# A fused long convolution and gated MLP: weights kept in an idle buffer, a complex product combined on VectorE, and whole-tile transfers

## Chip, cores, metric

One core of one Trainium2 chip runs the whole program. The metric is the device time of one execution in microseconds (us), lower is better. A profile is one execution; its span is about 2 us shorter than the time of the same execution. Runs are compared within one chip session, where kernel and kernel before alternate.

## The reference, cut to what matters

```python
# q, k, v: 1 x 2048 x 640 bf16; w_gate, w_up: 640 x 1728; w_down: 1728 x 640
x  = A_q
xn = layernorm(x)
k_shift = sum of 4 shifted copies of k, each times a weight per channel
kv = k_shift * v
y  = irfft(rfft(pad(kv)) * rfft(pad(ssm_k)))[:2048] + kv * ssm_D   # causal convolution of length 2048
glu = (sigmoid(xn @ w_gate) * (xn @ w_up)) @ w_down
out = x + xn * y + glu
```

The 2048 rows lie in the kernel as 16 row groups of 128 partitions (`acc[128, 16, 640]`). The gated MLP runs in four blocks of 512 rows: gate and up matmuls first, then the "down projection" of the block. The convolution is a Fourier transform in factors, all of them matmuls, done for ten channel steps, woven between the MLP's matmuls: first transform, second transform, a complex product in frequency on VectorE, third transform into a buffer V, and, after each five steps, a fourth transform out of V, whose result is multiplied with xn and added to `acc`.

## The kernel before

The instruction order is a fixed list made ahead of time (`ORDER`), so an edit of one operation leaves all others in their places. The parts that matter (cuts marked `# ...`):

```python
xq4 = A_q.flatten_outer_dims().rearrange("(n q m) d -> q n m d", q=4, m=NQ)   # 4 x 32 x 16 x 640
oq4 = out.flatten_outer_dims().rearrange("(n q m) d -> q n m d", q=4, m=NQ)

def load_x(q, m0, m1, eng, pri):            # a quarter of the partitions
    dma(lambda e: e.dma_start(acc[32 * q:32 * q + 32, m0:m1, :], xq4[q][:, m0:m1, :]), ...)

def store(m0, m1, pri, two=False):
    for q in range(4):
        dma(lambda e, q=q: e.dma_start(oq4[q][:, m0:m1, :], acc[32 * q:32 * q + 32, m0:m1, :]), ...)

def rec_prod(idx, pri):                     # X: spectrum of kv, H: of the filter; real part in partitions
    # ...                                   # 0-63, imaginary in 64-127; b = two halves of the step
    for h in range(2):                      # Q = X * (H with its halves swapped): four half products
        for b in range(2):
            a, o = slice(64 * h, 64 * h + 64), slice(64 - 64 * h, 128 - 64 * h)
            dve(... nc.vector.tensor_tensor(Q(b)[a], X(b)[a], H(b)[o], ALU.mult) ...)
    for b in range(2):                      # X = X * H
        dve(... nc.vector.tensor_tensor(X(b), X(b), H(b), ALU.mult) ...)

def rec_st3(idx, pri):                      # third transform: the sums and signs of the complex
    # ...                                   # product are in the two matrices A[0], A[1]
        nc.tensor.matmul(o, lhsT=tl[S_][:, b, 0, j, :], rhs=Ab[:, 0, :], start=True, stop=False)
        nc.tensor.matmul(o, lhsT=tl[Z][:, b, j, :], rhs=Ab[:, 1, :], start=False, stop=True)

for q in range(2):                          # first rows of x on two queues, SP and ACT
    load_x(q, 0, 1, "SP", FIX)
    load_x(q + 2, 0, 1, "ACT", FIX)
# ... rows 1-3 likewise; rows 4-7 and 8-15 later, four quarters each on SP
store(0, 8, 240.0); store(8, 12, 242.0); store(12, 14, 244.0); store(14, 15, 246.0); store(15, 16, 248.0)
```

Of the kernel before, what the change touches and what calls it, by code (L numbers as in the profile page):

```python
# [25 lines left out]
G = 4  # L26
# [16 lines left out]
def _dft_tables():  # L43
# [20 lines left out]
    A = np.zeros((2, K2, 2, N2, 2))  # L64
# [3 lines left out]
    A = A.reshape(P, 2, N2 * 2)  # L68
# [10 lines left out]
    6, 0, 5, 1, 4, 2, 8, 7, 11, 10, 13, 12, 9, 14, 3, 16, 71, 72, 15, 73, 74, 75, 17, 91, 86, 76, 77, 87, 81, 88, 19,  # L79
    78, 82, 64, 96, 79, 89, 83, 550, 97, 80, 90, 92, 84, 94, 147, 85, 93, 29, 98, 100, 99, 102, 101, 103, 148, 551,  # L80
    149, 150, 151, 154, 152, 63, 153, 156, 542, 155, 20, 157, 56, 543, 544, 546, 545, 24, 21, 547, 548, 27, 26, 552,
    549, 568, 553, 554, 556, 555, 57, 557, 558, 569, 560, 42, 559, 561, 562, 62, 564, 563, 23, 61, 565, 566, 32, 570,
    567, 572, 18, 571, 59, 574, 573, 104, 575, 586, 105, 578, 587, 106, 107, 588, 579, 576, 58, 108, 112, 582, 577,
    580, 43, 583, 111, 581, 30, 109, 589, 110, 25, 590, 584, 113, 39, 591, 593, 44, 45, 592, 132, 60, 134, 133, 22,
    594, 135, 596, 31, 585, 598, 597, 595, 600, 599, 602, 601, 604, 35, 603, 40, 605, 28, 36, 41, 158, 606, 159, 160,
    607, 37, 161, 610, 608, 609, 33, 611, 34, 38, 162, 612, 163, 164, 613, 171, 616, 628, 166, 615, 180, 614, 617,
    182, 181, 629, 618, 165, 622, 167, 168, 623, 66, 170, 177, 169, 65, 624, 179, 185, 172, 625, 67, 178, 174, 619,
    68, 627, 194, 626, 620, 621, 646, 630, 195, 196, 631, 632, 173, 647, 175, 197, 633, 634, 184, 199, 176, 47, 635,
    198, 183, 53, 636, 638, 200, 114, 50, 186, 639, 117, 46, 637, 54, 640, 201, 642, 49, 115, 187, 116, 51, 188, 191,
    641, 644, 643, 664, 193, 215, 189, 648, 192, 202, 649, 52, 190, 121, 214, 48, 650, 224, 203, 118, 665, 651, 119,  # L90
    652, 226, 225, 653, 213, 654, 136, 120, 205, 656, 655, 122, 129, 657, 216, 128, 69, 645, 227, 658, 218, 127, 217,
    95, 660, 228, 55, 659, 204, 661, 229, 219, 682, 662, 666, 220, 130, 244, 684, 206, 126, 243, 683, 668, 667, 663,
    207, 70, 246, 670, 669, 123, 247, 283, 124, 208, 290, 672, 288, 671, 230, 209, 289, 231, 287, 674, 125, 232, 286,
    233, 284, 675, 676, 234, 235, 210, 678, 211, 673, 677, 679, 212, 131, 680, 685, 221, 687, 686, 681, 223, 137,
    689, 138, 222, 688, 142, 245, 238, 717, 140, 690, 718, 248, 236, 239, 691, 693, 249, 237, 273, 139, 694, 143,
    250, 144, 145, 254, 141, 695, 255, 256, 696, 257, 697, 276, 698, 699, 258, 259, 700, 260, 275, 261, 240, 701,
    262, 242, 263, 702, 241, 274, 264, 705, 265, 703, 251, 704, 706, 146, 252, 253, 711, 303, 692, 712, 304, 305,
    713, 292, 277, 714, 278, 279, 294, 306, 293, 707, 716, 307, 295, 708, 280, 715, 308, 297, 266, 296, 268, 710,
    267, 298, 281, 719, 309, 269, 310, 720, 721, 311, 285, 709, 270, 312, 735, 723, 271, 313, 724, 314, 272, 722,
    725, 736, 727, 323, 726, 300, 729, 728, 301, 302, 282, 731, 324, 730, 333, 733, 291, 380, 732, 334, 335, 384,  # L100
    381, 737, 734, 753, 336, 739, 738, 338, 337, 383, 741, 299, 386, 740, 319, 743, 385, 742, 322, 320, 321, 387,
    745, 325, 330, 747, 744, 746, 331, 327, 326, 749, 332, 748, 328, 754, 317, 751, 391, 315, 329, 318, 390, 750,
    316, 349, 339, 356, 340, 755, 341, 400, 342, 757, 343, 756, 771, 402, 344, 772, 752, 759, 401, 806, 758, 389,
    347, 761, 392, 382, 345, 348, 394, 760, 346, 393, 395, 763, 762, 350, 396, 765, 420, 764, 419, 351, 388, 766,
    767, 352, 422, 773, 353, 423, 768, 769, 354, 357, 770, 774, 355, 358, 370, 776, 775, 359, 360, 778, 361, 777,
    403, 779, 781, 362, 780, 782, 405, 404, 783, 406, 377, 363, 407, 788, 378, 379, 789, 408, 371, 409, 790, 410,
    411, 372, 791, 373, 374, 784, 792, 793, 416, 375, 785, 417, 418, 794, 376, 427, 787, 795, 428, 429, 796, 786,
    421, 364, 797, 424, 365, 425, 800, 799, 367, 366, 412, 426, 368, 808, 807, 413, 449, 824, 414, 369, 810, 798,
    801, 415, 450, 452, 802, 453, 397, 803, 398, 399, 809, 451, 430, 804, 514, 811, 521, 805, 812, 432, 431, 813,
    814, 454, 460, 455, 825, 815, 816, 461, 462, 817, 818, 456, 433, 528, 819, 535, 820, 434, 435, 821, 822, 842,  # L110
    436, 437, 463, 438, 826, 439, 464, 440, 827, 465, 441, 823, 828, 442, 829, 444, 443, 830, 466, 445, 843, 467,
    831, 832, 468, 469, 446, 834, 470, 447, 471, 835, 448, 833, 836, 472, 837, 474, 473, 838, 475, 839, 840, 860,
    861, 476, 841, 844, 477, 478, 845, 846, 457, 847, 848, 458, 459, 849, 850, 482, 851, 852, 483, 484, 853, 854,
    862, 485, 855, 856, 486, 487, 857, 858, 488, 489, 479, 490, 863, 481, 480, 864, 865, 492, 498, 491, 866, 867,
    500, 499, 870, 868, 493, 869, 501, 859, 871, 502, 503, 872, 496, 494, 497, 876, 504, 495, 505, 877, 506, 507,
    873, 508, 878, 509, 510, 874, 875, 512, 511, 882, 513, 883, 536, 884, 537, 885, 538, 539, 879, 886, 887, 515,
    881, 880, 888, 540, 516, 541, 889, 517, 518, 905, 908, 890, 519, 907, 904, 891, 520, 906, 522, 903, 893, 892,
    909, 523, 902, 911, 524, 525, 910, 913, 526, 529, 912, 527, 530, 895, 894, 531, 532, 897, 533, 896, 534, 898,
    899, 900, 901
]  # L120
ON_DVE = [
    101, 134, 133, 135, 160, 181, 196, 226, 137, 138, 140, 139, 144, 256, 259, 253, 305, 302, 335, 337, 321, 360,
    404, 379, 374, 418, 429, 366, 399, 431, 462, 435, 478, 459, 484, 487, 480, 499, 503, 539, 518, 525, 532
# [93 lines left out]
def kernel(  # L217
# [42 lines left out]
    At = cst.tile([P, 2, 2 * N2], U16, name="At")  # L260
# [7 lines left out]
    eps = cst.tile([P, 1], F32, name="eps")  # L268
    st = cst.tile([P, 6, NQ], F32, name="st")
    eps2 = cst.tile([P, 1], F32, name="eps2")  # L270
# [6 lines left out]
    SLOTS = {"w": 4, "xq": 2, "xnT": 1, "sig": 2, "bs": 2, "kt": 1, "vt": 1, "ht0": 1, "ht1": 1, "kvt": 2,  # L277
# [12 lines left out]
    def make(b, tag, i):  # L290
        shape, dt = SHAPE[tag]
        if b.startswith("pst"):
            shape, dt = [P, NC, P], BF16
        if b.startswith("psT"):
            shape, dt = [P, 2, 1024], BF16
        if b in ("xk", "xv"):
            shape, dt = [P, 2, 2, 4 * DM // 2], BF16
        pool = ps if tag in ("c", "g") else wk
        return pool.tile(shape, dt, name=f"{tag}{i}", tag=f"{tag}{i}")
# [19 lines left out]
    def dma(fn, nd, run, q="SP", **kw):  # L319
        few = 1.4 if nd <= 64 and run > 1000 else 1.0  # L320
        plan.op({q: (0.48 + nd / 8000.0, lambda: fn(nc.sync if q == "SP" else nc.scalar))},
                size=few * nd * (10.6 + run / 23.8) / 16e3 + 0.03, **kw)

    def mm(n):
        return n / 2.4 + 3.0
# [4 lines left out]
               WDS=1.98, X1=22.54, X2=60.0, X3=84.74, LN1=40.0, LN2=80.0, LN3=90.0, WL=12.23, KV1=30.0,  # L330
               A1=53.98, LS1=55.48, LNS=70.0, EVB=-0.5, ST4=2.0, GP=2, H0=29.0, B0=64.19, SP=30.34)
# [15 lines left out]
    def load_x(q, m0, m1, eng, pri):  # L347
        dma(lambda e: e.dma_start(acc[32 * q:32 * q + 32, m0:m1, :], xq4[q][:, m0:m1, :]), 32, 1280 * (m1 - m0), q=eng,
            w=[("acc", m, q) for m in range(m0, m1)], pri=pri)

    def load_w(tr, n, pri):
        b = f"w{tr}_{n}"
        nb = max(0.0, pri - 14)
        kw = dict(pri=pri, nb=nb)
        if n == 6:
            dma(lambda e: e.dma_start(tl[b][:, :, 0:192], wgr[:, :, 1536:1728]), 640, 384, w=[(b, 0)], alloc=[(b, "w")], **kw)
            dma(lambda e: e.dma_start(tl[b][:, :, 256:384], wur[:, :, 1536:1664]), 640, 256, w=[(b, 1)], **kw)
            dma(lambda e: e.dma_start(tl[b][:, :, 192:256], wur[:, :, 1664:1728]), 640, 128, w=[(b, 2)], **kw)
            return
        f0, src = 512 * (n // 2), (wgr, wur)[n % 2]  # L360
        if tr == 0 and n < 2:
            for h in range(2):
                dma(lambda e, h=h: e.dma_start(tl[b][:, :, 256 * h:256 * h + 256], src[:, :, f0 + 256 * h:f0 + 256 * h + 256]),
                    640, 512, w=[(b, h)], alloc=[(b, "w")] if h == 0 else (), pri=pri + 0.5 * h)
# [520 lines left out]
```

## Time and profile before

| | kernel before |
|---|---|
| time, median of 3 | 277.43 us (276.89 to 512.8; the 512.8 is one stray execution) |
| span of the profiled execution | 279.1 us (that execution took 281.0) |
| TensorE busy / VectorE busy | 252.7 / 207.0 us |
| from the last matmul to the end | 12.3 us (10.9 in a second profile, taken later) |

How to read it: TensorE is busy for nearly the whole span, so what counts is each microsecond in which TensorE waits or has not yet begun or is already done. The prediction below prints the lines that carry this.

### The profile page before, as it was taken

The numbers are of one execution on the slowest core, as the hardware profiler recorded it, in microseconds if no ns is written. First come the engines' busy times: TensorE is split into PE (matmuls) and PEld (weight loads), VectorE is DVE, ScalarE is ACT, GpSimd is POOL, SyncE is SP. The second block draws the span as 40 slices with busy tenths as digits, with TensorE's granted clock in tenths as the row PEclk, the third lists the DMA queues.
The fourth block names the chain that finished last, engine by engine and source line by source line (L and its number), as shares of the span: only waits on it lengthen the run. The fifth ranks groups of instructions, "written<-read, shape, count | busy, mean of one in ns | idle before, by whom it ended". The sixth has DMA issues, their size and how long they took to land.

```text
span 279.1 us, 9682 instructions
## 1 busy us (share of the span) xinstructions
PE 252.7 (91%) x4344; PEld 156.5 (56%) x4380; DVE 207.0 (74%) x342; ACT 144.0 (52%) x214; POOL 0.7 (0%) x6
## 2 busy tenths in 40 slices
PE   8899887997799999999999999999999999999800
PEld 3754334774355547777456646667655555776500
DVE  5433147899489998869979998999888568864840
ACT  4642586133699979436557654224457754341100
POOL 1000000000000000000000000000000000000000
PEclk9999997999799999999999999999999999999965
DMA  7999999999769984999987602900464110000266
GB/s 181 265 234 290 193 202 192 152 273 256 148 132 338 193 218 115 166 216 152 250 168 209 162 2 67 295 25 5 116 194 167 44 31 2 2 2 2 63 132 188
DMA packets 94720, 42.17 MB, mean 151 GB/s; under 512 B 68432, under 2 KB 93592, under 8 KB 94360
## 3 DMA queue, kind: packets, MB, share of 16 engines
q1 hardware_dynamic: 94488, 41.24, 65.5%
q8 instruction: 34, 0.56, 0.9%
q10 hardware_dynamic: 192, 0.33, 0.4%
q14 instruction: 6, 0.05, 0.1%
HBM read 35.00 MB, written 5.24 MB: 144 GB/s over the span
## 4 chain that ended last, share of the span: by engine, by line
PE 83%; issue 4%; ACT 3%; DMA 3%; DVE 2%; SPq 1%; DVEq 0%; ACTq 0%
PE g L730 34%; PE g L745 23%; PE c L514 8%; PE c L582 4%; PE c L493 3%; PE c L552 3%; PE c L551 3%; DMA acc<-in_A_q_dram 3%; PE g L775 2%; PE g L710 2%; ACT jk L615 1%; ACT jk L621 1%; ACT xnT L312 1%; SPq L366 0%; DVE xq L652 0%
## 5 line engine op out<-in xcount | busy, mean ns | idle before, releaser
L730 PE MATMUL g<-xnT,w 128*128 128x512 bf16 x484 | 116.3, 384 | 4.6 <-issue 2.1
L730 PEld LDWEIGHTS <-w 128*128 128x128 bf16 x520 | 48.5, 99 | 56.8 <-issue 3.3
L745 PE MATMUL g<-wd,hT 128*128 128x320 bf16 x448 | 67.7, 304 | 0.1
L698 DVE TENSOR_TENSOR hT<-sig,g 128x512 bf16<-128x512 bf16 x52 | 35.4, 687 | 25.8 <-PE g L730 17.8
L745 PEld LDWEIGHTS <-hT 128*128 128x128 bf16 x448 | 42.4, 99 | 17.3 <-issue 0.4
L696 ACT ACTIVATE sig<-g 128x512 bf16<-128x512 f32 x52 | 30.8, 596 | 27.8 <-PE g L730 26.1
L312 ACT CAST S<-c 128x1024 bf16<-128x1024 f32 x25 | 24.8, 1012 | 21.8 <-PE c L514 21.8
L536 DVE TENSOR_TENSOR P<-S 64x1024 bf16<-64x1024 bf16 x40 | 27.4, 686 | 8.2 <-PE c L552 3.7
L514 PEld LDWEIGHTS <-Mt 64*128 64x128 f16 x1280 | 19.9, 95 | 10.5 <-issue 9.3
L312 ACT CAST V<-c 128x1024 bf16<-128x1024 f32 x20 | 19.4, 1013 | 11.5 <-PE c L552 11.5
L514 PE MATMUL c<-T,Mt 64*128 64x64 bf16 x1280 | 22.3, 190 | 2.9 <-issue 2.9
L313 DVE CAST S<-c 128x1024 bf16<-128x1024 f32 x15 | 18.3, 1223 | 5.5 <-PE c L514 5.4
L315 ACT ACTIVATE T<-c 128x1024 bf16<-128x1024 f32 x14 | 13.9, 1022 | 15.6 <-PE c L493 15.6
L551 PE MATMUL c<-At,S 128*128 128x128 f16 x160 | 19.3, 219 | 0.0
L552 PE MATMUL c<-At,P 128*128 128x128 f16 x160 | 19.3, 219 | 0.0
L312 ACT CAST T<-c 128x1024 bf16<-128x1024 f32 x14 | 13.8, 1014 | 10.6 <-PE c L493 10.5
L551 PEld LDWEIGHTS <-S 128*128 128x128 bf16 x160 | 15.6, 98 | 1.3 <-DVE S L539 0.2
L552 PEld LDWEIGHTS <-P 128*128 128x128 bf16 x160 | 15.6, 98 | 1.2
L756 DVE TENSOR_TENSOR acc<-g,acc 128x320 bf16<-128x320 f32 x32 | 14.5, 485 | 0.9 <-PE g L745 0.7
L458 DVE TENSOR_TENSOR tb<-kt,sT 128x1024 bf16<-128x1024 bf16 x20 | 13.7, 687 | 0.7 <-ACT kt L312 0.6
L463 DVE TENSOR_TENSOR ta<-ta,tb 128x1024 bf16<-128x1024 bf16 x20 | 13.8, 688 | 0.3
L539 DVE TENSOR_TENSOR S<-S 128x1024 bf16<-128x1024 bf16 x20 | 13.1, 688 | 0.3
(76 smaller groups left out, 196.1 us busy)
## 6 DMA issues: line engine op xcount, KB each, us to landing
w<-in_B_w_gate_dram SPq DMA_DIRECT2D x11, 640.0 KB, 4.8
w<-in_B_w_up_dram SPq DMA_DIRECT2D x11, 640.0 KB, 6.8
kt<-in_A_k_dram SPq DMA_DIRECT2D x8, 320.0 KB, 7.6
vt<-in_A_v_dram SPq DMA_DIRECT2D x8, 320.0 KB, 7.1
xnd<-xq SPq DMA_DIRECT2D x4, 640.0 KB, 7.5
ht<-in_A_ssm_k_dram SPq DMA_DIRECT2D x16, 96.0 KB, 6.3
wd<-in_B_w_down_dram SPq DMA_DIRECT2D x3, 480.0 KB, 5.5
acc<-in_A_q_dram SPq DMA_DIRECT2D x4, 320.0 KB, 7.3
```

What stands on the lines that cost most here:

```text
L312: fa = lambda: nc.scalar.copy(out=out_fn(), in_=in_fn())
L313: fd = lambda: nc.vector.tensor_copy(out_fn(), in_fn())
L315: fa = lambda: nc.scalar.activation(out_fn(), in_fn(), ACT.Copy, scale=scale)
L514: nc.tensor.matmul(tl[cs[e]][:, b, 64 * kk:64 * kk + 64], lhsT=Mb[rows, k, 64 - 64 * r:192 - 64 * r], rhs=tl[T][rows, 2 * k + r].rearrange ...
L536: dve(n, 2, lambda a=a, o=o, b=b: nc.vector.tensor_tensor(Q(b)[a], X(b)[a], H(b)[o], ALU.mult), r=sr + ([(Z, b, 0)] if h else []), w=[(Z, ...
L551: nc.tensor.matmul(o, lhsT=tl[S_][:, b, 0, j, :], rhs=Ab[:, 0, :], start=True, stop=False)
L552: nc.tensor.matmul(o, lhsT=tl[Z][:, b, j, :], rhs=Ab[:, 1, :], start=False, stop=True)
L696: act(512, lambda: nc.scalar.activation(tl[sg][:], tl[cs[0]][:], ACT.Sigmoid), r=[(cs[0],)], w=[(sg,)], alloc=[(sg, "sig")], pri=pri - 2000)
L698: dve(512, 1, lambda: nc.vector.tensor_tensor(hT[:, fc, :], tl[sg][:], tl[cs[1]][:], ALU.mult), r=[(cs[1],), (sg,)], w=[(hk, fc)], pri=pri ...
L730: nc.tensor.matmul(tl[c][:], lhsT=tl[wb][:, k, o:o + P], rhs=tl[X][:, k, :], start=(k == 0), stop=(k == NC - 1))
L745: nc.tensor.matmul(tl[pd[i]][:, 0:320], lhsT=hT[:, fc, t4 * P:(t4 + 1) * P], rhs=wd[:, fc, 320 * i:320 * i + 320], start=(fc == 0), stop=( ...
L756: dve(320, 1, lambda i=i, m=m, pd=pd: nc.vector.tensor_tensor(acc[:, m, 320 * i:320 * i + 320], tl[pd[i]][:, 0:320], acc[:, m, 320 * i:320 ...
```

## The change

Its intent, in five parts:

1. **Third transform halved.** VectorE forms the real and imaginary part of the product itself, so one matmul with a third matrix is enough: 160 matmuls less on TensorE, 40 "combining" instructions more on VectorE.
2. **VectorE relieved elsewhere.** In seven of ten steps two DMAs swap H's halves, so that four half products become two full ones; 18 gate products get their up value copied out of PSUM by ScalarE first.
3. **Weights kept.** The first block's gate and up weights stay on chip for the second block, four of their seven pieces in the buffer V. V is then free for the third transform only when the second block is done, and the order moves the second and third transforms back.
4. **Another end.** The last down block stands after the fourth transform and is split by column halves.
5. **Transfers joined.** Each load and store of `acc` is one DMA over 128 partitions in place of four over 32.

The core of the diff (the two order tables, the single-slot second transform and bookkeeping of keys are cut):

```diff
-    A = np.zeros((2, K2, 2, N2, 2))
+    A = np.zeros((2, K2, 3, N2, 2))
+    A[0, :, 2, :, 0], A[0, :, 2, :, 1] = c, s
+    A[1, :, 2, :, 0], A[1, :, 2, :, 1] = -s, c
 ...
-    def load_x(q, m0, m1, eng, pri):
-        dma(lambda e: e.dma_start(acc[32 * q:32 * q + 32, m0:m1, :], xq4[q][:, m0:m1, :]), 32, ...
+    def load_x(m0, m1, eng, pri):
+        dma(lambda e: e.dma_start(acc[:, m0:m1, :], xq4[:, :, m0:m1, :]), P, ...
+    def weight(tr, n):
+        tr = 0 if tr == 1 else tr
+        if tr == 0 and n < 4:
+            return ("wv", n), lambda: tl["wv"][:, n]        # lies in the slot of V
 ...
+        if idx in PRM["SWAP"]:                              # steps 3 to 9
+            for h in range(2):
+                dma(... tl[Z][a] <- tl[S_][o, :, 1] ...)    # H with its halves swapped
+            for b in range(2):
+                dve(... nc.vector.tensor_tensor(Q(b), X(b), Q(b), ALU.mult) ...)
 ...
+        if idx in PRM["ZC"]:                                # all ten steps
+            for b in range(2):
+                dve(... nc.vector.tensor_tensor(X(b)[0:64], X(b)[0:64], X(b)[64:P], ALU.subtract) ...)
+                dve(... nc.vector.tensor_tensor(X(b)[64:P], Q(b)[0:64], Q(b)[64:P], ALU.add) ...)
 ...
-   nc.tensor.matmul(o, lhsT=tl[S_][:, b, 0, j, :], rhs=Ab[:, 0, :], start=True, stop=False)
-   nc.tensor.matmul(o, lhsT=tl[Z][:, b, j, :], rhs=Ab[:, 1, :], start=False, stop=True)
+   nc.tensor.matmul(o, lhsT=tl[S_][:, b, 0, j, :], rhs=Ab[:, 2 if zc else 0, :], start=True, stop=zc)
 ...
+            parts = ([(0, 7, (0,)), (7, 14, (0,)), (0, 7, (1,)), (7, 14, (1,))] if last else ...
 ...
-    def store(m0, m1, pri, two=False):
-        for q in range(4):
-            dma(lambda e, q=q: e.dma_start(oq4[q][:, m0:m1, :], acc[32 * q:32 * q + 32, m0:m1, :]), 32, ...
+    def store(m0, m1, pri, d0=0, d1=DM):
+        dma(lambda e: e.dma_start(oq4[:, :, m0:m1, d0:d1], acc[:, m0:m1, d0:d1]), P, ...
 ...
-    store(15, 16, 248.0)
+    store(15, 16, 247.0, d1=320)
+    store(15, 16, 248.0, d0=320)
```

## The prediction

> **What bounds the kernel now.** I read the engine totals and slices first, then the chain of waits, the groups, the tail in order of time, and last the order in which both kernels place their instructions.
>
> ```profile
> PE 252.7 (91%) x4344; PEld 156.5 (56%) x4380; DVE 207.0 (74%) x342; ACT 144.0 (52%) x214; POOL 0.7 (0%) x6
> ...
> PEclk9999997999799999999999999999999999999965
> ...
> PE 83%; issue 4%; ACT 3%; DMA 3%; DVE 2%; SPq 1%; DVEq 0%; ACTq 0%
> ```
>
> TensorE carries 83% of the chain that ended last, so it is the bound; VectorE is second with 74%. The clock row shows two dips, near 45 and 72 us. A busy PE is not yet an efficient one, so I added up its work at the measured pace, from the end of the first block (14.65 us) on: gate/up 520 x 0.216 = 112.2 us, down 448 x 0.136 = 60.8, first transform 9.7, second 20 x 1.04 = 20.8, third 320 x 0.056 = 17.8, fourth 16 x 0.62 = 9.9, small ones 1.6; in all 232.8. TensorE ends at 266.8, so 252.1 us passed and 19.3 were lost: 11.6 of them before the 195th gate/up matmul (91.2 us). Those are the gaps at 29, 35, 40, 43 and 45 us (3.4), one of 2.92 at 68.25, and 9% of clock over 40 to 80 us (3.6); the rest is small. From 91 to 208 us (the 435th gate/up matmul) TensorE had 116 us of work in 117.
>
> ```profile
> L536 DVE TENSOR_TENSOR P<-S 64x1024 bf16<-64x1024 bf16 x40 | 27.4, 686 | 8.2 <-PE c L552 3.7
> L313 DVE CAST S<-c 128x1024 bf16<-128x1024 f32 x15 | 18.3, 1223 | 5.5 <-PE c L514 5.4
> L551 PE MATMUL c<-At,S 128*128 128x128 f16 x160 | 19.3, 219 | 0.0
> L552 PE MATMUL c<-At,P 128*128 128x128 f16 x160 | 19.3, 219 | 0.0
> L539 DVE TENSOR_TENSOR S<-S 128x1024 bf16<-128x1024 bf16 x20 | 13.1, 688 | 0.3
> ```
>
> These are the parts that the change touches: two matmuls per channel step in the third transform, and the complex product on VectorE. The 219 ns is one matmul's latency; 32 of them run from 243.11 to 244.90 us, 0.056 each.
>
> ```profile
> 259.35 16.29 SPq L598 DMA_DIRECT2D out_dram<-acc  x20
> ...
> 263.97 0.84 PE L582 MATMUL c<-V,Bt 32*32 32x80 bf16 x63 [0.75 <-ACT kt L312]
> ...
> 266.12 0.69 PE L582 MATMUL c<-V,Bt 32*32 32x80 bf16 x65 [1.32 <-issue]
> ...
> 268.70 0.82 DVE L591 TENSOR_TENSOR acc<-acc,vt 128x1280 bf16<-128x1280 bf16 x1
> ```
>
> The tail: TensorE stops at 266.8 and the last VectorE add at 269.5, yet the span is 279.1. Twenty stores, of 32 partitions each, leave one queue in order until 275.6, and the last needs 2.4 us to land. So 12.3 us follow the last matmul.
>
> **What the Trainium skill says.** "TensorE: Matmul & The Clock Gate", Back-to-back issue gap, gives N/2.4 + 2.5 ns, 56 ns at 128 columns; the trace has 0.056 us, so a matmul taken out is worth that, not 219 ns. "VectorE: DVE Perf Modes", The perf-mode tier table, says that a bf16 product reaches 2x from SBUF and 1x from PSUM; the trace agrees: 1024 columns from SBUF take 686 ns and 512 from PSUM 687. The same page, Two Vector instructions with no wait between them, says that an instruction whose inputs start in different quadrants of partitions waits for all earlier ones. The trace agrees: plain 1024-column products start every 0.60 us (128.43, 129.03, 129.63), four L536 half products, whose two inputs lie in different halves, take 2.83, so 0.71 each.[...]
>
> **Part 1, the third transform.** It goes from 320 matmuls to 160: 160 x 0.056 = 8.9 us off TensorE, which is the bound. The price is on VectorE: 40 half-partition combining operations with inputs in different halves, 40 x 0.71 = 28.4 us.
>
> **Part 2, relief for VectorE.** Counted in the two instruction orders: in 7 of 10 steps a copy by DMA swaps the halves, so 28 half products become 14 full ones: 28 x 0.71 - 14 x 0.60 = 11.5 us off. The S casts on VectorE go from 15 to 2, against three V casts more: 10 x 1.14 = 11.4 off (start to start). 18 gate products read SBUF in place of PSUM; from 819 ns at 1280 columns and 687 at 1024 I get 0.52 ns a column and so 0.42 us for 512, an estimate, which saves 18 x 0.26 = 4.8, less 0.7 for one copy. Small casts and norms give some 2 us back and take as much. Net 28.4 - 11.5 - 11.4 - 4.1 = +1.4: VectorE stays near 208 us. ScalarE gains 13 S casts (13.2), 17 copies (10) and loses some V casts: 144 to about 165 us, still no bound.
>
> **Part 3, weights kept.** Seven loads, 4.4 of 42.2 MB, vanish from the second block. But only 0.8 us of TensorE's waiting names a weight load, so directly it is worth about 1 us. It costs order: V is free for the third transform only after the second block. The first third-transform matmul moves from behind gate/up matmul 200 to behind 250, and the second transform starts behind 195 in place of inside the first down projection. The same convolution work must fit into less time. Of the 11.6 us lost early I expect 8 to stay; the 2.92 gap names no releaser, so I do not take all of it off.
>
> **Part 4, the middle, where I expect the new bound.** Between gate/up matmuls 195 and 435 the new order has, on VectorE: 61 key-value operations x 0.60 = 36.6, 15 gate products 9.0, 11 short ones 3.9, 12 half products 8.5, 25 full ones 15.5, 28 combining 19.6, 13 casts 14.8, 16 down adds 6.7, the fourth transform's 10 operations 7.9, small 0.9: 123.4 us. Before, the same stretch held 106.7 (in 117, 91%). TensorE there has 117.8 us plus about 25 switches from the second transform back to gate/up at the 0.16 us that the timeline shows: 122. The two engines are level, and neither can then be quite full. I take 96% of the longer: 128 us. Single-slot second transforms (32 matmuls, one PSUM slot, one cast) let this interleave; they change no work.
>
> **Part 5, the end.** The last 56 down matmuls (7.6 us) now stand after the fourth transform, whose stalls (2.2 us in the last 4.7) and adds no longer close the kernel, and stores are 6 in place of 20. After the last matmul remain one add 0.49, an issue 0.43, landing 2.4 and the close 1.1, with waits 4.6 us in place of 12.3: 7.7 off.
>
> **Sum.** Up to gate/up matmul 195: start 14.65 + work 60.1 (42.1 gate/up, 15.2 down, 1.3 first transform, 1.5 small) + 8 lost = 82.7. Middle 128: 210.7. From there TensorE has 45.9 us and I allow 3 for the fourth transform's stalls: 259.6. End 4.6: span 264.2. The profiled span of before was 279.1 against a median of 277.43 unprofiled, so 1.7 less: 262.5, rounded up to 263, 5% faster.
>
> **Rivals.** (a) TensorE stays the only bound: the middle takes 122 and early loss falls to 5. Then 254. For it: before, TensorE was 99% full there with VectorE at 91%. Against: VectorE now has 16% more to do in it. (b) VectorE becomes a hard bound, because the swap copies arrive late. A 320 KB read back takes 4.0 us here, and the swap (two of 256 KB on the one in-order queue) stands between the last cast and the product; if VectorE waits 1.5 us in each of 7 steps, the middle takes 138: 272, near no gain. For: queue waits of 12 and 36 us exist in that queue. Against: two S buffers, and next step's eight key-value products can fill the time. (c) The early part is bound by DMA anyway (busy share around 1.0 up to 60 us) and nothing is won before 83 us: +3, 266. (d) Tail alone: the parts in the middle cancel (8.9 off TensorE against VectorE's load) and only 8 to 10 us of the end remain: 268.
>
> **Range and chances.** The tail's 7.7 us and the 8.9 off TensorE are counted, not argued; the middle's filling is the wide term, from -6 to +10. Range 255 to 271. Faster by over 2% means under 271.9: 0.88. Within 2%: 0.11. Slower by over 2%: 0.01, only if the swaps or one wait stall everything.
>
> **What would show it.** Third transform: 160 matmuls, about 9 us of start-to-start time. VectorE busy 203 to 213, ScalarE 160 to 170. VectorE's share in 85 to 210 us above 92% while TensorE shows gaps ended by it (S casts, combining products); gate/up matmul 435 near 211. After the last matmul under 5.5 us. Wrong if VectorE idles on the swap copies, if gate/up 195 comes after 88 us, or if TensorE remains 99% full in the middle.

## More of the kernel before

For the kernel before, the rows that touch `acc` (destination and source, queue, count, size of one, median time from issue to landing in us):

```profile
acc<-in_A_q_dram SPq DMA_DIRECT2D x4, 320.0 KB, 7.3
out_dram<-acc SPq DMA_DIRECT2D x4, 320.0 KB, 5.5
acc<-in_A_q_dram SPq DMA_DIRECT2D x4, 160.0 KB, 7.2
...
acc<-in_A_q_dram ACTq DMA_DIRECT2D x2, 120.0 KB, 3.5
acc<-in_A_q_dram ACTq DMA_DIRECT2D x2, 40.0 KB, 2.0
acc<-in_A_q_dram SPq DMA_DIRECT2D x2, 40.0 KB, 1.8
```

All of `acc` goes in and out in quarters of 32 partitions, and the slowest group lands in 7.3 us. The page's DMA row (40 slices of the span, busy tenths of the 16 DMA engines) is

```profile
DMA  7999999999769984999987602900464110000266
```

It begins with 7 tenths, and its last two slices, in which little but stores runs, have 6.

## The result and the profile after

| | before | after |
|---|---|---|
| time, median | 277.62 us (4 runs) | 315.5 us (4 runs, 312.58 to 318.69) |
| ratio of fast runs | | 1.134, 95% interval 1.124 to 1.144 |
| span of the profiled execution | 279.1 us | 316.8 us |

A ratio is the mean time of one kernel's fast runs over the mean of the other's in the same rounds, so not quite the ratio of the medians. The profiled execution of after (318.69 us) counts as slow, being 2% above the fastest; I use its trace only for differences far larger than that. The prediction, 263 us and 88% for faster, was wrong in sign: by the means of the fast runs (314.5 against 277.4 us) the kernel is 37 us slower.

From the page of after, engine totals and the DMA row:

```profile
PE 260.8 (82%) x4220; PEld 153.9 (49%) x4220; DVE 206.4 (65%) x359; ACT 163.1 (51%) x241; POOL 0.7 (0%) x6
...
DMA  4699959725996537668979878121374520012221
```

VectorE's 206.4 and ScalarE's 163.1 us lie inside the predicted 203 to 213 and 160 to 170: the count of engine work was right. What differs is the row's two ends. It begins with 4 tenths in place of 7, and in the last slices, where only stores run, 2 tenths or fewer are busy in place of 6. The waits of after (engine, line and tile, what it waited for: us in all, times, longest):

```profile
ACT jk L642 <- DMA acc<-in_A_q_dram: 31.7, 3, 15.2
...
DVE bs L635 <- DMA acc<-in_A_q_dram: 11.8, 1, 11.8
...
PE c L701 <- DVE xq L679: 7.1, 1, 7.1
```

Three engines wait, directly or through one another, for the loads of x. In order of time (start, duration, engine, what, and in brackets the idle time before it and what ended that), the start, the load of rows 8 to 15, and the end:

```profile
15.76 0.72 PE L701 MATMUL c<-ident,xq 128*128 128x128 bf16 x5 [7.14 <-DVE xq L679]
...
53.74 0.57 SPq L355 DMA_DIRECT2D acc<-in_A_q_dram  x1
...
54.87 19.95 SPq L425 DMA_DIRECT2D kt<-in_A_k_dram  x2
...
74.83 0.74 ACT L642 ACTIVATE jk<-acc 128x640 bf16<-128x640 bf16 x1 [15.17 <-DMA acc<-in_A_q_dram]
...
282.80 25.64 SPq L626 DMA_DIRECT2D out_dram<-acc  x5
...
292.01 0.49 DVE L795 TENSOR_TENSOR acc<-g,acc 128x320 bf16<-128x320 f32 x1 [0.46 <-PE g L783]
```

The first matmul on data starts at 15.76 us, where before had it at 7.73. One load of 1280 KB, issued at 53.74, is there at 74.83: 21 us, 62 GB/s. In the kernel before a quarter of 320 KB landed in 7.3 us; in the same place of the new order, with the load cut in four (first experiment), the four are issued from 36.93 us on and all there at 49.74, 12.8 us. Meanwhile the next two issues on the same queue take 19.95 us to leave it (8.90 us with the transfers cut in four, first experiment). And after the last add at 292.5 the kernel still stores for 24 us. A stretch of that end (columns: stretch, length, busy us and count of PE, PEld, DVE, ACT and POOL, granted clock, DMA share, GB/s):

```profile
300.00:316.00 16.00, 0.00 (x0) 0.00 (x0) 0.00 (x0) 0.00 (x0) 0.00 (x0) 0.50 0.21 76
```

A share of 0.21 is that of a bit under 4 of 16 engines. A count of the raw trace's packets agrees: the commonest number under way at once is 4 in this stretch, and 16 in the end of the kernel before (268 to 277 us). The access pattern of these DMAs on the memory side is 4 x 32 x rows x 640: its slowest dimension is 4. The Trainium skill states what follows from that, in "DMA: Bandwidth & Descriptors", Why a DMA increments its semaphore by 16 and not by 1: the number k of engines that a DMA runs on is the largest k up to 16 that divides the slowest dimension, other than one of size 1, of both access patterns. For 4 and 128 that is 4; for the old quarters, with 32 and 32, it is 16. The share of 0.21 agrees with k = 4.

A table of stages, read from the traces, says where the 37.7 us of span came from. Marks are the starts of the four down projections, the end of the last matmul and the end of the span. "quads" is after with its transfers of `acc` cut in four again (first experiment):

| stage (length in us) | before | after | quads |
|---|---|---|---|
| start to down projection 0 | 45.4 | 58.8 | 47.7 |
| to down projection 1 | 62.4 | 61.3 | 52.0 |
| to down projection 2 | 65.4 | 69.1 | 68.0 |
| to down projection 3 | 65.8 | 76.5 | 76.3 |
| to the last matmul | 27.8 | 26.3 | 27.8 |
| to the end | 12.3 | 24.8 | 5.2 |
| span | 279.1 | 316.8 | 277.0 |

After minus quads is 11.1, 9.4, 1.1, 0.2, -1.5 and 19.6 us: the cost sits where x is loaded and where the result is stored, and nowhere else.

### The profile page after: what moved, and what is told of

It reads as the page before. It is cut to its first block, busy times and chain, and to the rows that moved or that the text cites. A ratio compares the mean times of both kernels' runs of the same rounds, so it can differ in the third digit from the quotient of the medians.

```text
span 316.8 us, 9407 instructions
## 1 busy us (share of the span) xinstructions
PE 260.8 (82%) x4220; PEld 153.9 (49%) x4220; DVE 206.4 (65%) x359; ACT 163.1 (51%) x241; POOL 0.7 (0%) x6
## 5 line engine op out<-in xcount | busy, mean ns | idle before, releaser
L765 PE MATMUL g<-xnT,w 128*128 128x512 bf16 x380 | 90.9, 385 | 5.8 <-ACT sig L729 5.1
L765 PEld LDWEIGHTS <-w 128*128 128x128 bf16 x380 | 34.8, 99 | 43.8 <-issue 8.3
L317 ACT CAST S<-c 128x1024 bf16<-128x1024 f32 x38 | 38.1, 1022 | 13.5 <-PE c L525 13.5
L731 DVE TENSOR_TENSOR hT<-sig,g 128x512 bf16<-128x512 bf16 x34 | 23.1, 685 | 25.7 <-ACT sig L729 16.0
L765 PE MATMUL g<-xnT,V 128*128 128x512 bf16 x140 | 33.0, 394 | 1.3 <-ACT sig L729 0.8
L729 ACT ACTIVATE sig<-g 128x512 bf16<-128x512 f32 x34 | 20.5, 603 | 17.2 <-PE g L765 9.4
L525 PEld LDWEIGHTS <-Mt 64*128 64x128 f16 x1280 | 21.6, 97 | 12.4 <-issue 11.2
L642 ACT ACTIVATE jk<-acc 128x640 bf16<-128x640 bf16 x13 | 9.6, 735 | 31.9 <-DMA acc<-in_A_q_dram 31.7
L765 PEld LDWEIGHTS <-V 128*128 128x128 bf16 x140 | 14.0, 101 | 18.5 <-issue 4.0
L609 PE MATMUL c<-V,Bt 32*32 32x80 bf16 x1024 | 11.4, 207 | 4.1 <-DVE T L318 1.6
L562 DVE TENSOR_TENSOR S<-S 64x1024 bf16<-64x1024 bf16 x20 | 13.7, 687 | 0.7
L564 DVE TENSOR_TENSOR S<-P 64x1024 bf16<-64x1024 bf16 x20 | 13.8, 689 | 0.5
## 6 DMA issues: line engine op xcount, KB each, us to landing
wd<-in_B_w_down_dram SPq DMA_DIRECT2D x3, 480.0 KB, 19.6
```

The lines of the kernel that those rows point to most:

```text
L317: fa = lambda: nc.scalar.copy(out=out_fn(), in_=in_fn())
L525: nc.tensor.matmul(tl[c][:, b, 64 * kk:64 * kk + 64], lhsT=Mb[rows, k, 64 - 64 * r:192 - 64 * r], rhs=tl[T][rows, 2 * k + r].rearrange("p ...
L562: dve(n, 2, lambda b=b: nc.vector.tensor_tensor(X(b)[0:64], X(b)[0:64], X(b)[64:P], ALU.subtract), r=[(S_, "p", b)], w=[(S_, "z", b)], pri ...
L564: dve(n, 2, lambda b=b: nc.vector.tensor_tensor(X(b)[64:P], Q(b)[0:64], Q(b)[64:P], ALU.add), r=[(S_, "z", b), (Z, b, 0)], w=[(S_, "q", b) ...
L729: act(512, lambda: nc.scalar.activation(tl[sg][:], tl[cs[0]][:], ACT.Sigmoid), r=[(cs[0],)], w=[(sg,)], alloc=[(sg, "sig")], pri=pri - 2000)
L731: dve(512, 1, lambda: nc.vector.tensor_tensor(hT[:, fc, :], tl[sg][:], tl[cs[1]][:], ALU.mult), r=[(cs[1],), (sg,)], w=[(hk, fc)], pri=pri ...
```

## The experiments

Seventeen kernels ran. A result is given as median us, and ratio to the kernel before with its 95% interval. Numbers of different sessions are compared by ratio; a "point" is 0.01 of it, some 2.8 us. Some variants compute a wrong result; that is said each time. The record's own check passed every version, these too, so "right" and "wrong" follow here from the edit and not from the check.

### 1. Cut the transfers in four again

Theory: four-engine transfers cost the 37 us. Rival: the new order of the convolution does, and waiting for loads is only where it shows.

```diff
-  e.dma_start(acc[:, m0:m1, :], xq4[:, :, m0:m1, :])
+  [e.dma_start(acc[32 * q:32 * q + 32, m0:m1, :], xq4[q][:, m0:m1, :]) for q in range(4)]
-  e.dma_start(oq4[:, :, m0:m1, d0:d1], acc[:, m0:m1, d0:d1])
+  [e.dma_start(oq4[q][:, m0:m1, d0:d1], acc[32 * q:32 * q + 32, m0:m1, d0:d1]) for q in range(4)]
```

Both edits:

> The kernel after, with its x loads and its output stores each cut into four DMAs by groups of 32 partitions, as the kernel before has them; nothing else is changed. Theory A (each whole-tile x load and store runs on 4 of the 16 DMA engines, because the slowest dimension of its DRAM side is 4): the start loses its 7.1 us wait, the 21 us load of 1280 KB shrinks to under 9, the time after the last matmul falls from 24 us to 5 to 7, and the time comes to 260 to 270 us. Rival B (the new order of work on VectorE and the late convolution cost the time): 300 us or more, with VectorE waits in the middle unchanged. Rival C (the same bytes on a busy memory, however they are cut): within 5 us of 315.

Only the loads:

> The kernel after with only the x loads cut into four. Theory A: the first transpose starts at 8 to 10 us in place of 15.8, ScalarE's 31.7 us of waiting on x fall below 6, and the tail stays at 22 to 26 us: 280 to 292 us. Rival C: 310 or more.

Only the stores:

> The kernel after with only the stores cut into four. Theory A: the start is as slow as in the kernel after, the time after the last matmul falls from 24 us to 5 to 7: 293 to 300 us. Rival C: 310 or more. If the two halves of the fault are independent, the two gains add up to that of quad_both within 4 us.

| kernel | median us | ratio to before |
|---|---|---|
| after | 315.5 | 1.134 (1.124 to 1.144) |
| loads cut | 297.33 | 1.075 (1.067 to 1.083) |
| stores cut | 297.16 | 1.072 (1.062 to 1.082) |
| both cut | 277.88 | 1.004 (0.996 to 1.013) |

The medians of the kernel after and of the stores-only version contain one slow run each. By the means of the fast runs (314.5, 297.4, 296.6 and 277.9 us) cutting the loads takes 17.2 us off, cutting the stores 17.9, and both 36.6: the costs add within 1.5 us, and together they are all of the loss. The theory stands, though two of its ranges were missed: both cut (260 to 270 us forecast) and loads cut (280 to 292) came in higher. The kernel with both cut is only level with before, 15 us from the prediction, so a second question is open: where is the expected gain?

### 2. The reverse: join the transfers in the kernel before

The edit, put in words:

```diff
-  four DMAs acc[32 * q:32 * q + 32, m0:m1, :] <- xq4[q][:, m0:m1, :], and four stores likewise
+  one DMA   acc[:, m0:m1, :] <- xq4[:, :, m0:m1, :], and one store likewise
```

> The kernel before with its four x loads of each group, and its four stores of each group, joined into one DMA as in the kernel after; nothing else. Theory A: slower by 20 to 45 us (300 to 320), with the first matmul on real data several us later and a tail of over 20 us. Rival B: within 5 us of 277.

Measured: 305.85 us (303.83 to 358.57), ratio 1.103 (1.092 to 1.114). The joining alone costs 28 us in a kernel that has nothing else of the change. Why it costs less there than the 37 us here, no run separates. Its profile fell on the 358.57 execution, with a clock of 0.73, and is not used.

### 3. First loads on two queues again

In the repaired version all first quarters leave on one queue per row group; before used SP and ACT for both. This and all later variants start from it; I call it **the repaired kernel**.

```diff
+  [(nc.scalar if q > 1 and m0 < 4 else nc.sync).dma_start(acc[32 * q: ...], xq4[q][...]) for q in range(4)]
```

> quad_both, and the first two x loads (blocks 0 and 1 to 3) again issued half from the SP and half from the ScalarE queue, as the kernel before has it. In quad_both the first transpose waited 3.8 us for the first x tile, and the first real matmuls began at 13.3 us against 9.0 before. If that is the queue's serial issue, the start comes back to 9 to 10 us and the time to 273 to 275. If the start is not on the path (the loads behind it set the pace), it stays at 277 to 278.

Measured: 275.88 us, ratio 0.994 (0.989 to 0.999). The first gate matmul moved from 13.31 to 9.55 us. The median is 2.0 us lower and the ratio 1.0 point, but the two intervals overlap, so that some of it reached the end is likely and not shown (273 to 275 us was forecast). Its stages against those of the kernel before (second profile, span 277.6; columns as in the stretch above). Kernel before:

```profile
45.78:107.74 61.96, 58.15 (x760) 34.11 (x760) 53.29 (x96) 40.58 (x70) 0.00 (x0) 0.97 0.95 203
107.74:173.15 65.41, 65.41 (x1308) 40.88 (x1305) 57.35 (x88) 36.91 (x46) 0.00 (x0) 1.00 0.78 158
173.15:238.72 65.57, 65.53 (x1310) 40.55 (x1305) 55.33 (x76) 32.88 (x39) 0.00 (x0) 1.00 0.35 95
238.72:266.75 28.03, 25.81 (x753) 19.35 (x751) 18.65 (x28) 7.59 (x11) 0.00 (x0) 0.99 0.10 25
266.75:277.60 10.85, 0.00 (x0) 0.00 (x0) 2.47 (x3) 0.66 (x1) 0.00 (x0) 0.50 0.79 187
```

Repaired kernel:

```profile
42.09:95.73 53.64, 52.17 (x611) 29.30 (x609) 39.84 (x84) 42.15 (x73) 0.00 (x0) 1.00 0.80 160
95.73:165.10 69.37, 66.34 (x1156) 39.78 (x1154) 62.56 (x99) 46.50 (x58) 0.00 (x0) 0.98 0.85 168
165.10:241.12 76.02, 70.79 (x1560) 42.87 (x1559) 64.62 (x98) 45.44 (x58) 0.00 (x0) 0.98 0.41 103
241.12:268.77 27.65, 23.89 (x641) 16.09 (x639) 16.79 (x26) 4.96 (x7) 0.00 (x0) 0.94 0.37 91
268.77:274.30 5.53, 0.01 (x1) 0.00 (x0) 0.49 (x1) 0.00 (x0) 0.00 (x0) 0.74 0.14 37
```

The second stage is 8.3 us shorter, the end 5.3. The two stages between are 4.0 and 10.5 us longer. Six of the 8.3 are TensorE work that was not saved but moved back (58.15 to 52.17 us busy). In the two longer stages TensorE idles 3.0 and 5.2 us where before it idled 0.0, while VectorE holds 62.6 and 64.6 us in place of 57.4 and 55.3. So the gain was given back in the middle. The waits there (timeline of the repaired kernel, 185 to 204 us) name VectorE and a swapped copy, and ScalarE where the third transform waits for a free PSUM slot:

```profile
185.98 0.69 DVE L550 TENSOR_TENSOR P<-S,P 128x1024 bf16<-128x1024 bf16 x1 [0.65 <-DMA P<-S]
...
193.18 0.69 PE L506 MATMUL c<-Ft,kvt 32*128 32x64 f16 x30 [0.54 <-DVE xq L318]
...
195.65 1.15 PE L610 MATMUL c<-V,Bt 32*32 32x80 bf16 x120 [0.43 <-DVE T L318]
...
197.67 1.20 PE L578 MATMUL c<-At,S 128*128 128x128 f16 x16 [0.86 <-ACT xq L317]
...
203.51 1.24 PE L766 MATMUL g<-xnT,w 128*128 128x512 bf16 x5 [0.78 <-DVE acc L796]
```

### 4. What the combining costs, and what the halving is worth

Take the 40 combining instructions out and leave the single matmul (wrong result, everything else in place):

```diff
-  dve(n, 2, lambda b=b: nc.vector.tensor_tensor(X(b)[0:64], X(b)[0:64], X(b)[64:P], ALU.subtract), ...
-  dve(n, 2, lambda b=b: nc.vector.tensor_tensor(X(b)[64:P], Q(b)[0:64], Q(b)[64:P], ALU.add), ...
+  dve(n, 2, lambda b=b: None, ...        # both
```

> quad_two_queues with the 40 combining operations on VectorE left out; the result is wrong on purpose. VectorE loses 28 us, TensorE nothing. Theory V (VectorE's queue bounds the stretch between gate/up matmuls 195 and 435, which took 136 us in quad_both where I had predicted 128): 8 to 15 us faster than quad_two_queues, and the gaps of TensorE that end with T casts on VectorE vanish. Theory P (TensorE with its switches between small blocks is the bound): less than 4 us faster.

Measured: 267.9 us, ratio 0.967 (0.960 to 0.974). 8.0 us less than the repaired kernel in the same session. Stages of this version:

```profile
95.76:161.39 65.63, 64.99 (x1155) 39.22 (x1153) 51.39 (x81) 46.25 (x58) 0.00 (x0) 1.00 0.88 177
161.39:234.16 72.77, 70.36 (x1561) 43.26 (x1560) 51.17 (x79) 45.78 (x58) 0.00 (x0) 0.98 0.43 107
```

VectorE loses 11.2 and 13.5 us of work in the two middle stages, and they get 3.7 and 3.3 us shorter; TensorE's idle time falls to 0.6 and 2.4. The rest of the 8 us lies in the last stage and the end. Between gate/up matmuls 195 and 435 the idle time of TensorE that VectorE ends falls from 5.4 to 0.6 us, as theory V said. The mean granted clock in that stretch was also higher in this profile (0.99 against 0.98), so a part of the gain, 1 to 2 us by an estimate from these two figures, may be clock.

Put the saved matmuls back instead, by issuing each third-transform matmul twice (result right, because the second overwrites the first with the same):

```diff
+  nc.tensor.matmul(o, lhsT=tl[S_][:, b, 0, j, :], rhs=Ab[:, 2 if zc else 0, :], start=True, stop=zc)
```

> quad_two_queues with every matmul of the third transform issued twice (the same result, written twice): TensorE +8.9 us, VectorE unchanged. Theory P: 7 to 10 us slower. Theory V: less than 4 us slower, since TensorE waits in that stretch anyway.

Measured: 279.44 us, ratio 1.007 (1.000 to 1.014), 3.6 us more than the repaired kernel. So with VectorE this full, 8.9 us of TensorE work weigh 3.6.

Both at once, no combining and twice the matmuls, which is the load of the old third transform in the new order (wrong result):

> zc_free with the third transform's matmuls doubled: the work of the third transform and the product as in the kernel before (320 matmuls, no combining), in the new order; wrong result on purpose. zc_free is 8.0 us faster than quad_two_queues, doubling the matmuls there cost 3.6. If the halving pays by itself in this order, this kernel is slower than quad_two_queues (275.9). Theory V says that it is 1 to 5 us faster: the 8.9 us of TensorE are worth less than the 28 of VectorE. With TensorE now the bound, I expect 267.9 + 6 to 8: 272 to 276.

Measured: 277.04 us, ratio 0.997 (0.992 to 1.001), against 0.994 (0.989 to 0.999) for the repaired kernel. The intervals overlap and the difference is 0.3 points: trading 160 matmuls for 40 combining instructions is worth about 1 us, give or take 2. (The forecast, 272 to 276 us and faster than the repaired kernel, missed.) From the version without combining to this one are 3.0 points, 8.3 us, nearly the full 8.9 of the matmuls: once VectorE is relieved, added matmuls cost almost all of their time.

Undo the trade in five of ten steps (0, 2, 6, 7, 9), result right:

```diff
-  ZC=(0, 1, 2, 3, 4, 5, 6, 7, 8, 9)
+  ZC=(1, 3, 4, 5, 8)
```

> quad_two_queues with the change's third transform undone in 5 of 10 steps (0, 2, 6, 7, 9; there two matmuls again and no combining; the right result): TensorE +4.5 us, VectorE -14 us. Theory V: 0 to 5 us faster than quad_two_queues. Theory P: 3 to 5 us slower.

Measured: 275.33 us, ratio 0.993 (0.987 to 0.999): the same as the repaired kernel. (A full undo with a right result was not run.)

### 5. The swapped copies

Without the copies, wrong result (the full product reads the unswapped H):

```diff
-  dma(lambda e, a=a, o=o: e.dma_start(tl[Z][a] ..., tl[S_][o, :, 1] ...), ...
+  dma(lambda e, a=a, o=o: None, ...
-  nc.vector.tensor_tensor(Q(b), X(b), Q(b), ALU.mult)
+  nc.vector.tensor_tensor(Q(b), X(b), H(b), ALU.mult)
```

> quad_two_queues without the 14 copies that swap halves; the full products read the unswapped half, so the result is wrong on purpose. VectorE's instructions are the same in number and length. VectorE waited 3.4 us on these copies (4 waits) in the third stage of quad_two_queues. If the copies' latency matters (rival b of the prediction): 3 to 8 us faster. If other work fills the time: less than 2 us.

Measured: 271.41 us, ratio 0.978 (0.973 to 0.982); 1.6 points below the repaired kernel, some 4.5 us. That is what the copies cost. In the repaired kernel VectorE waits 4.3 us for them (five waits, 1.4 us at most), so it is probably the waiting; but the 3.7 MB that they move went away with them, and no run separates the two.

Half products in all steps and no copies, result right:

```diff
-  SWAP=(3, 4, 5, 6, 7, 8, 9)
+  SWAP=()
```

> quad_two_queues with the half products of the kernel before in all ten steps, no copies; right result. VectorE + 14 x 0.71 x 2 - 14 x 0.60 = +11.5 us. Theory V (VectorE bounds the middle): 2 to 6 us slower; the waits on copies that vanish give some back. If VectorE did not bound: the same within 1 us.

Measured: 280.66 us, ratio 1.010 (1.003 to 1.017). So the copies are worth their waiting: without them the kernel is again 1.6 points slower.

### 6. Both VectorE terms at once

The prediction is 13 us below the repaired kernel; combining (8.0) and the copies (4.5) would make 12.5 if they added. Both edits of 4 (first) and 5 (first), wrong result:

> The two-queue repair of the changed kernel without the 40 combining instructions and without the half-swapped copies (wrong result on purpose). Dropping the combining alone took 8.0 us off (275.9 to 267.9), dropping the copies alone 4.5 (to 271.4). Theory A, what is missing between 275.9 and the predicted 263 is these two added terms of work and latency on the same VectorE chain: the gains add, 262 to 265 us. Rival B, both hide the same wait (V is busy with the weights until block 1 ends, so the convolution is late anyway): the gains do not add, 266 to 268 us.

Measured: 266.04 us, ratio 0.962 (0.958 to 0.965). They do not fully add: 2.7 and 1.6 points would make 4.3, and 3.2 are measured. After the combining is gone, the copies are worth 0.5 points, 1.5 us, and the intervals overlap. Theory A is missed by 1 us and the time is at the edge of rival B's range. That both terms feed one wait, that of TensorE for VectorE in the middle, fits this; B's own reason, V busy with the weights, was not tested. The stage after down projection 2, 65.6 us in the kernel before, is

```profile
159.60:231.33 71.73, 67.57 (x1549) 41.97 (x1559) 51.55 (x79) 45.32 (x58) 0.00 (x0) 1.00 0.28 74
```

still 6 us longer, with less VectorE load than before (51.6 against 55.3) and more matmuls in it (1559 weight loads against 1305): that fits work moved back and now simply carried out. (Ten matmul records of this stage are missing, so TensorE's idle time in it is not read.) About 3 of the 13 us are left, and they are not in the kernel: this version's span is 264.0 us, the predicted span 264.2. The prediction went from span to time by taking 1.7 us off, because it set the span of one execution (279.1; that execution took 281.0) against the median of others. In the profiles here an execution takes about 2 us more than its own span (265.8 against 264.0 in this one), so its own sum meant some 266 us. That the spans agree so closely is partly chance: the table near the end shows terms that miss in both directions.

### 7. The kept weights

Put most of the saved traffic back (3.9 of 4.4 MB): six copies of 640 KB of weights from device memory to device memory in block 1, in the places of the old loads. The result stays right.

```diff
+  if tr == 1 and fc % 4 == 0 and fc < 12:
+      nc.sync.dma_start(spare[(fc // 4, u)][:], (wgr, wur)[u][:, :, fk:fk + 512])
```

> The two-queue repair with six copies of 640 KB of the weights from device memory to device memory added in block 1, in the places where the weights of block 1 were loaded before; the result stays right. Prediction's view, that the saved reload is worth about 1 us because nothing waited for those loads: 275.5 to 277 us, and the stretch from the first to the second down projection stays within 1 us of 53.6. Rival, that this stretch is 8.8 us shorter than before (53.6 against 62.4) because the weights are not loaded: 279 to 285 us, the stretch 57 to 62.

Measured: 275.06 us, ratio 0.993 (0.987 to 0.999): no loss. The stretch concerned, down projection 0 to 1:

```profile
42.77:94.74 51.97, 51.37 (x602) 29.23 (x609) 39.56 (x84) 42.50 (x73) 0.00 (x0) 1.00 0.99 234
```

It moves 234 GB/s in place of 160, has its DMA engines full (0.99), and is no longer than without (53.64). So the traffic was free; nothing waits for these copies, so what waiting for reloaded weights would cost is not tested. Of the 8.3 us by which this stretch is shorter than before, 6.0 are the matmul work that the order puts elsewhere; the rest is less idle time, of open origin.

### 8. Stores in two

To test the rule for k at another point: stores of two pieces of 64 partitions, slowest dimension 2.

```diff
+  [e.dma_start(oq4[2 * h:2 * h + 2, :, m0:m1, d0:d1], acc[64 * h:64 * h + 64, m0:m1, d0:d1]) for h in range(2)]
```

> quad_two_queues with every store cut in two by 64 partitions, so that the slowest dimension of its DRAM side is 2. Theory A in its strict form (a DMA runs on as many engines as the largest number up to 16 that divides the slowest dimension of both sides; and always the same first ones): both halves share 2 engines, the mean busy share of the 16 engines in the tail is 0.12 (4 of 16 gave 0.21 to 0.25 in the kernel after), they move 35 to 45 GB/s in place of 76, and the kernel takes 315 to 345 us. Rival D (one large store is slow because it is one: two of half the size lie between one and four): 280 to 290 us.

Measured (one round of two runs): 315.11 us, ratio 1.134. The end:

```profile
290.00:312.00 22.00, 0.00 (x0) 0.00 (x0) 0.00 (x0) 0.00 (x0) 0.00 (x0) 0.50 0.12 45
```

0.12 is 2 of 16 engines, and 45 GB/s against 76 with four, as if the two halves of a store, and one store and the next, shared the same two. With one DMA per store and the loads cut the time was 297.33 us (first experiment), so twice as many DMAs are slower still: not their number but the slowest dimension decides. A single DMA with the 32 as its slowest dimension has no run: it would step over partitions in the second dimension.

### 9. The new end by itself, and a control

The kernel before with a new end like that of the change, not quite the same (14 down matmuls stand after its last fourth transform, 56 in the change, whose stores are all on SP): last down block split by halves among and after the last fourth transforms, six of the last stores' quarters moved to the ACT queue.

```diff
+  parts = ([(0, 7, (0,)), (7, 14, (0,)), (0, 7, (1,)), (7, 14, (1,))] if last else ...
+  store(15, 16, 248.0, d1=320)
+  store(15, 16, 249.0, two=True, d0=320)      # and two=True for rows 0-7 and 8-11
```

> The kernel before with only the end of the change put in: the last down block split by column halves and placed among and after the last fourth-transform units, its store in two halves, and the stores of rows 0 to 11 and of the last half issued half on the ACT queue (the last 20 stores of before took 16.3 us to issue one after another on SP). Theory, the end's 12.3 us from the last matmul to the end of the span is due to order and queue and has nothing to do with the convolution's new form: 271 to 275 us, a tail of 5 to 7.5 us, and then this is the fastest right kernel. Rival, the tail is bound by landing and not by issue: 276.5 to 278 us.

Measured: 276.27 us, ratio 1.000 (0.994 to 1.005): no gain, and above the theory's range. Its profile has 6.6 us after the last matmul, as the theory said, but its last stage is 30.5 us in place of 28.0 (27.8 in the first profile). It is not more work: both have the same 753 matmuls. What differs is the granted clock, 0.89 in place of 0.99; for 6.8 us of that stage it was 0.50:

```profile
237.15:267.63 30.48, 28.39 (x753) 20.12 (x751) 20.53 (x30) 8.25 (x11) 0.00 (x0) 0.89 0.17 38
260.50:267.30 6.80, 6.02 (x147) 3.48 (x145) 5.07 (x7) 1.01 (x2) 0.00 (x0) 0.50 0.52 113
```

The repaired kernel has such a stretch in its last stage too (0.50 from 257.8 to 261.2 us), the two profiles of the kernel before have none between 76 and 266 us. Why the clock drops there is not shown. The SP queue is still busy with stores to the end (18 issues in 13.9 us):

```profile
257.52 13.89 SPq L596 DMA_DIRECT2D out_dram<-acc  x18
```

So the microseconds saved after the last matmul cannot be read as a gain by themselves. To see how much of the long end was the profiled execution's own, the kernel before, unchanged, as a control:

> The kernel before unchanged, as a control: its first profile was of an execution of 281.0 us, 3.6 us longer than its timed median of 277.4, so a part of the differences by stage may be that execution's. Theory, the end's 12.3 us was the execution's too: time 277 to 278 us, ratio within 0.005 of 1, and a tail of 6 to 9 us in the new profile. Rival, the tail is the kernel's: 11 to 13 us again, and the excess lies in the stages before.

Measured: 278.73 us, ratio 1.007 (0.999 to 1.015), span 277.6. The last matmul ends at the same time within 0.1 us in both profiles (266.75 and 266.81); the end is 10.9 us in place of 12.3. My theory of 6 to 9 us is wrong: the long end is the kernel's, with some 1.4 us of it differing between the two executions. And the ratio of a kernel to itself can be 1.007, so single differences under about 1% above are not to be trusted.

Last, the half-undone version of 4 with its late stores on two queues (result right):

```diff
+  (nc.scalar if q > 1 and m0 in (8, 14, 15) else e).dma_start(oq4[q]...)
```

> The version with half of the third-transform change undone (275.3 us) with the late stores of rows 8 to 11, 14 and 15 issued half on the ACT queue, the result right. If the last issues on SP (some 0.64 us each, one after another) end the span, 1 to 2 us less: 273 to 274.5 us, and the fastest right kernel. If the landing of the last store ends it: 275 to 276 us.

Measured: 277.51 us, ratio 1.005 (0.993 to 1.016): nothing gained, within the noise.

No version with a right result beats the kernel before by 2%; the best, 0.993 and 0.994, are inside what the control allows.

## Why the prediction was wrong, step by step

**The step that failed** is in Part 5, "stores are 6 in place of 20", with its counterpart in the sum, "start 14.65", taken over unchanged. I counted issues, gave the last store a landing of 2.4 us, that of a 40 KB quarter, and asked of no DMA how many engines it would run on. The joined transfers run on 4 of 16. The end became 24.8 us in place of the predicted 4.6; cutting only the stores gave 17.9 us back. The start and the load of rows 8 to 15 cost another 17.2. The two add to 35.1; undone together they gave 36.6 of the 37 us. No rival named a transfer getting slower, so no part of the range held this; 1% for "slower" was far too little.

The other terms can be read where the transfers are cut in four (marks by matmul starts, in us):

| term | predicted | both cut | repaired kernel |
|---|---|---|---|
| start to gate/up matmul 195 | 82.7 | 81.9 | 77.9 |
| gate/up matmul 195 to 435 | 128 | 135.8 | 136.9 |
| from there to the last matmul | 48.9 | 54.1 | 53.9 |
| end | 4.6 | 5.2 | 5.5 |
| span | 264.2 | 277.0 | 274.3 |

**Part 1, third transform.** The 160 matmuls are there and are worth what was counted once VectorE is relieved (8.3 us measured, 8.9 counted). But 40 combining instructions cost 8.0, so that the trade is worth about 1 us, within the noise. The prediction named their price on VectorE, 28.4 us, and still booked the 8.9 as "counted, not argued".

**Part 2, VectorE's relief.** The total was right (206.4 against "near 208"), and ScalarE's too (163.1 against 165).

**Part 3, weights kept.** "About 1 us": 0 within the noise for the traffic, and the price in order was named. That matmul 195 comes at 81.9 us, near the predicted 82.7, is chance: with the first loads on two queues again it comes at 77.9, so less was lost early than the 8 us expected, as rival (a) said. (In after itself it comes at 102.3.)

**Part 4, the middle.** The counts of work were right, in the stretch and not only in total: VectorE 124.4 us in the repaired kernel against 123.4 predicted, and TensorE's matmuls there, counted at the prediction's pace, 117.9 against 117.8. What failed is the step from there, "96% of the longer: 128 us". The stretch in the kernel before (second profile) and in the repaired kernel:

```profile
90.90:210.80 119.90, 119.86 (x2323) 75.07 (x2322) 108.29 (x173) 68.45 (x90) 0.00 (x0) 1.00 0.69 154
77.93:214.87 136.94, 128.78 (x2627) 77.92 (x2626) 124.39 (x195) 87.64 (x110) 0.00 (x0) 0.98 0.64 141
```

TensorE idled 8.2 us, 5.4 of them ended by VectorE and 2.8 by ScalarE, where 6 were allowed. The larger part of the miss is that it was busy 128.8 us where 122 were counted. A lower granted clock (0.98 against 1.00) is some 3 us of that, an estimate from these two figures; the rest is open. The reading of before was off as well: its stretch took 119.9 us, not 117, because matmul 435 comes at 210.8 us and not at 208 (36 matmul records are missing from the first trace). Without the combining and the copies (experiment 6) VectorE has 106 us there and the stretch takes 129.0 us, so most of the excess goes with them. Rival (b), VectorE as the hard bound with late copies, named 138 and 272 us. It was close for the middle, but it assumed 1.5 us of waiting in each of 7 steps, and 4.3 us in all were seen.

**Part 5, the end, apart from the transfers.** With the stores cut it is 5.2 us, predicted 4.6. As a gain over before it is worth less than the 7.7 us counted: a similar end put alone into the kernel before gave nothing that could be measured, and in its profile the last stage, with the same matmuls at a lower clock, took back more than half of the time saved.

So of the 52 us between prediction and result 37 come from counting transfers without a look at their access patterns. Of the other 15, about 2 went with the first loads' queue (not clear of the noise), 10 are the sum's own for the repaired kernel (+8.9 in the middle, +5.0 after it, -4.8 before it, +0.9 at the end), and 3 are the wrong step from span to time.

## What to carry to other kernels

Before joining DMAs, look at the slowest dimension of both access patterns: four transfers of 32 partitions used all 16 engines, one of 128 partitions with a memory side of 4 x 32 used four, and the difference was 13% of the kernel. When a change trades work from the busiest engine to the second, even a right count of both in the stretch that matters is not enough: here 8.9 us saved on one cost 8.0 on the other, which only taking each out by itself showed. And a shorter end in a profile is not yet a gain: read the stretch before it too, its clock included (here 4.3 us less at the end, 2.5 more before it).

## What the Trainium skill lacked or had wrong

- The rule for k is not lacking. "DMA: Bandwidth & Descriptors" has it in Why a DMA increments its semaphore by 16 and not by 1, and its table Rules for kernel authors tells planners that an outermost dimension below 16 confines a DMA to at most that many engines; I missed both. The runs confirm it (slowest dimension 4: DMA share 0.21, 76 GB/s; 2: 0.12, 45 GB/s). Its section Bandwidth has the rule to batch DMAs to at least 1 MiB and does not say there that this presumes all 16 engines: the 1280 KB load took 21 us on four, its four 320 KB quarters together 12.8 us.
- No page that I read gives what a slow transfer does to those behind it on its queue: two 320 KB issues after the 1280 KB load took 19.95 us to leave the SP queue, 8.90 us after its quarters.
- No page that I read helps to judge two engines that are both nearly full: in the two middle stages of the repaired kernel, with VectorE at 90% and 85%, TensorE idled 3.0 of 69.4 and 5.2 of 76.0 us.
